# When the triangles of the delta rule are prepared: grams one group sooner, from key copies of their own, and inversion steps spread over three chunks

## The chip, the cores and the metric

The kernel runs on one core of one Trainium2 chip. The metric is the device time of one execution in microseconds (us); the table below gives the median of three runs. A core has five engines that work beside each other and wait for each other by semaphores: TensorE (PE in the profile; PEld its weight loads), VectorE (DVE), ScalarE (ACT), GpSimd (POOL) and SyncE (SP), which here only issues DMAs. Each engine takes its own instructions in order.

## The reference

Four batches of eight heads and 768 tokens (head size 48) go through the delta rule, token by token:

```python
k_n = k / (np.linalg.norm(k, axis=-1, keepdims=True) + 1e-06)
for t in range(S):
    kt, vt, bt = (k_n[:, :, t], v[:, :, t], beta[:, :, t, None])
    y[:, :, t] = np.einsum('bhd,bhde->bhe', q[:, :, t], state)
    v_old = np.einsum('bhde,bhd->bhe', state, kt)
    state = state + bt[:, :, :, None] * np.einsum('bhd,bhe->bhde', kt, vt - v_old)
```

Its result, 3072 tokens of 384 features, goes through two feed-forward layers with 2048 hidden units each: `h = x @ w_in`, a function of h (first a clipped square that becomes linear above 1, then the square of `max(h, 0)`), and `g @ w_out`. All is float32.

## The kernel before, in words

**Chunks.** The 768 tokens are cut into 24 chunks of 32 tokens; a chunk holds all batches and heads. With K the keys of a chunk, Q its queries and S the state, a chunk needs `W`, the inverse of a unit lower triangle made of `K K'`, scaled. Then U = W (diag(n) V − K S), Y = Q S + strictlower(Q K') U, and S grows by K' U. On TensorE these are six *steps*, each a burst of small matmuls: ks (K S), tr (times W), yy (Q S, line 406), sps (K' U into the state), yy again (times U, line 440) and xt (the transpose of Y for the next layer).

**Grams and triangles.** What a chunk needs before its state is known is made ahead. `gram` (line 260) computes K K' and Q K' on TensorE, and VectorE masks them into the tile `gp` (line 284). Four chunks form a *group* (0 to 5). When a group has its four grams, `tri` (line 317) inverts its 128 triangles at once, one on each partition: VectorE transposes `gp` into `gm` (line 325), a few small instructions make norms and factors, two larger ones (lines 350 and 354, each in halves on VectorE and GpSimd) prepare `gm` and `tx`, then 30 *steps* follow, each a product (`t`, line 370) and a sum (`tx`, line 376). For groups 1 to 5 all 60 are on GpSimd. A closing transpose on VectorE (line 380) puts the result into `gp`, from which tr reads it.

**The layers.** The first layer takes the chunks in nine *blocks* of 2 or 3 chunks (256 or 384 columns), the second in eight blocks of 3. A block has 16 *hidden units* of 128, each with nine matmuls `h` and nine matmuls `acc` two units later. Between the two, ScalarE and VectorE make of h the function's value and split it in a high and a low part. For each unit that is `r` (line 516), `g` (line 518) and `gl` (line 527) on VectorE, with ScalarE's `gh` (line 526) between the last two. Beside that VectorE, ScalarE and GpSimd convert weights that come as float64 bits: those of the first layer in block 0, those of the second in the later blocks (lines 158 to 164).

**What sets the order.** Each block has 32 *slots*, two for a hidden unit. The steps of a later block's chunks are spread evenly over the slots of the block before (`put_a`), and after certain steps of chunk c come grams of chunks some way ahead, read from the same key tiles (`kqt`, a ring of 6) that the chunk's own steps read later. When a group's last gram is in slot a, its triangle begins in slot a + 1; its steps are recorded in the 6 slots (`PACE`) from a + 6, and the closing transpose in the slot where the group's first chunk starts. All this is inside `manual_schedule(engines=ENGINES)` with TensorE alone in `ENGINES`: TensorE's instructions stay in the order in which they are recorded, those of the other engines are put in order by a scheduler of the language, when the kernel is built.

**Loads.** All DMAs are issued by SP, in order: keys and queries (`kqt`, two DMAs a chunk), keys and values (`kv`, ring of 3), weights (`raw`), the converted second weights out to memory (`w2f`) and, in the last block, back in (`w2r`, in the same ring as `kqt`). A chunk's values are multiplied by norms on GpSimd (`value`, line 249).

Of the kernel before, what the change touches and what calls it, by code (L numbers as in the profile page):

```python
# [8 lines left out]
F32 = mybir.dt.float32  # L9
# [9 lines left out]
# Chunks of the blocks in which the first layer takes them  # L19
SIZES = [2, 2, 3, 3, 3, 3, 3, 2, 3]  # L20
# and of the groups whose triangles are inverted together
GROUPS = [4] * 6
# [3 lines left out]
def kernel(  # L26
# [9 lines left out]
    """The delta rule in chunks of T tokens, with keys as they come (K, not normalised):  # L36
    with n = |k| + 1e-6 and g = beta / n**2,
        W = inverse(1 + diag(g) strictlower(K K')) diag(g),  U = W (diag(n) V - K S),
        Y = Q S + strictlower(Q K') U,                       S <- S + K' U.
    Its result goes through the two feed-forward layers, whose float32 products are sums of  # L40
    products of exact parts: x = hi + lo, 12 bits each (float32r).

    kq:   [chunk, (batch % 2, feature), (batch // 2, head, key tokens | query tokens)]
    kv:   [chunk, (batch, token), (key | value, head, feature)]
    beta: [(batch, chunk of the group, head), group, token]
    w1, w2: [128 hidden, in | out, partition, column], the bits of float64
    out:  [chunk, (batch, token), feature]
    """
# [12 lines left out]
    GC = T // H               # chunks of a full group  # L61
    NM = NCH // NC            # blocks of the second layer
    N = NC * P
    LAG = 2
    LENT = 28                 # weights whose bits may lie in the last weights' place
    RG = 3
    RAW = 3
    WT, WL = 3, 4
    GB = 2
    MANY = 4                  # first hidden units that may use the chunks' banks  # L70
    HEAD = 8                  # slots of the first block without steps of the second's chunks
# [17 lines left out]
    def weight(i, f):  # L89
        """(hi, lo) of hidden units f's weights: in (i = 0), out (1)."""  # L90
        if (i, f) not in pairs:
            t = wp.tile([P, 2, DM], F32R, tag=f"w{i}{f}", name=f"w{i}{f}")
            pairs[i, f] = t[:, 0], t[:, 1]
        return pairs[i, f]
# [3 lines left out]
    # Until the first layer begins, its banks serve the chunks too.  # L98
# [18 lines left out]
    def load_kq(c, tag="kqt", bufs=6):  # L117
        if c >= NCH:
            return
        t = kqt[c] = ring.tile([P, B2, H, 2 * T], F32, tag=tag, bufs=bufs, name="kqt")  # L120
        for o in range(2):
            nc.sync.dma_start(
                t[64 * o:64 * o + D].rearrange("p b h x -> p (b h x)"), kq[c, D * o:D * (o + 1)]
            )

# [6 lines left out]
    # A weight comes as the bits of a float64: words (low, high).  The high word, read as a  # L132
    # float32 and scaled by 2**-112, has its exponent rebiased; shifted left by 3 it is the
    # weight's leading 21 bits as a float32.  The low word adds the last 3 bits, rounded to
    # nearest, but never up into the leading ones.
    raws = {}

    # The last weights' place takes some of the first ones' bits.
# [8 lines left out]
    # The second layer's weights become float32.  # L147
# [22 lines left out]
    # The first layer's become their two parts, x = hi + lo.  # L170
# [14 lines left out]
    def weight_items(w):  # L185
        # A hidden unit's second weights are needed LAG units after its first.
        keys = [(w, f, i) for f in range(NF) for i in range(2)]
        if w == 0:
            keys.sort(key=lambda k: (k[1] + LAG * k[2], -k[2]))

        def item(x):
            _, f, i = keys[x]
            box = {}
            if w == 0:
                r = part_stages(keys[x], box)
            else:
                r = convert_stages(keys[x], box)
                r.append(lambda: nc.sync.dma_start(w2f[f, :, i], box["t"]))
            s1 = r[1]
            r[1] = lambda: (s1(), ahead(x + 1))  # L200
            return r

        # Loads run ahead of the conversions by the buffers there are.
        todo = list(enumerate(keys))

        def ahead(x):
            end = x + RAW
            if w == 0 and end < LENT:
                end = min(end + 2, LENT)
            while todo and todo[0][0] < end:  # L210
                load_w(*todo.pop(0))

        return lambda: ahead(0), [item(x) for x in range(len(keys))]
# [3 lines left out]
    def fetch_w2(f):  # L217
        w2r[f] = ring.tile([P, 2, DM], F32, tag="kqt", bufs=6, name="w2r")
        nc.sync.dma_start(w2r[f], w2f[f])
# [14 lines left out]
    def norm_stages(ss, sm):  # L234
        """n = sqrt(ss) + 1e-6, the root after one Newton step."""
        return [
            lambda: nc.scalar.activation(sm[0], ss, AF.Sqrt, scale=0.25, bias=tiny),
            lambda: nc.vector.reciprocal(sm[2], sm[0]),
            lambda: nc.vector.scalar_tensor_tensor(
                sm[1], ss, 0.25, sm[2], ALU.mult, ALU.mult),  # L240
            lambda: nc.vector.scalar_tensor_tensor(
                sm[0], sm[0], 1e-6, sm[1], ALU.add, ALU.add),
            lambda: nc.vector.reciprocal(sm[2], sm[0]),
        ]

    def value(c):
        """V becomes diag(n) V."""
        g, j = group_of[c]
        nc.gpsimd.tensor_mul(  # L249
            kvt[c][:, 1], kvt[c][:, 1],  # L250
            nt[g][:, j * H:(j + 1) * H].rearrange("p (h o) -> p h o", o=1)
            .to_broadcast([P, H, D]),
        )
# [6 lines left out]
    def gram(c, lo=0, hi=2, late=0):  # L260
        """K K' (x = 0) and Q K' (x = 1), x from lo to hi; what is returned is left to do
        (if late > 1, to what left its bank)."""
# [5 lines left out]
        g = att([P, H, hi - lo, T], "g")  # L268

        def one_(b, h, p, pd):  # L270
            x = kqt[c][pd, b // 2, h]
            nc.tensor.matmul(  # L272
                g[p, h].rearrange("p x i -> p (x i)"), x[:, 0:T], x[:, lo * T:hi * T],
                start=h == 0, stop=True, skip_group_check=True,
            )

        per_bh(one_)

# [16 lines left out]
    # The keys of the first chunks with the keys and queries of those after them, up to the  # L295
    # last of the first block: these do without a state.
# [13 lines left out]
    # The upper triangle of a chunk's K K', one (batch, chunk, head) a partition; its diagonal  # L310
    # is |k|**2.  x[c, i] becomes W[i, c], each of `parts` (engine, rows) by itself.
# [77 lines left out]
    us = {}  # L389

    def chunk_steps(c):
# [4 lines left out]
        def of_state(o, x):  # L396
            """K S (x = 0) or Q S; at first, S is the sum of K' U so far."""
# [32 lines left out]
        def qs():  # L430
            o = t["o"] = att([P, H, D], "yy")
            of_state(o, 1)
            if c >= HEADS:
                kqt.pop(c)
                load_kq(c + 6)
# [24 lines left out]
        def done():  # L460
            """Of ku and xt, the second makes room."""
            t["n"] = t.get("n", 0) + 1
            if t["n"] == 2:
                del kvt[c]
                load_kv(c + 3)
# [20 lines left out]
    def prods(pairs, swap=False):  # L486
        """Sums of hi hi + lo hi + hi lo, the right's lo last."""
# [11 lines left out]
    def hidden(layer, n, f):  # L499
# [12 lines left out]
        if layer == 0:  # L512
            # g = (min(relu(h + 1), 2) / 2)**2 + relu(h - 1)
# [69 lines left out]
    def flow(items, lag=1):  # L583
        """The stages of items, each item `lag` steps behind the one before it."""
# [20 lines left out]
    PACE = 6  # L605
# [9 lines left out]
    with tc.manual_schedule():  # L615
# [4 lines left out]
        load_kq(4)  # L620
        load_kq(5)
# [27 lines left out]
        for c in range(HEADS):  # L649
            load_kq(c + 6)  # L650
# [9 lines left out]
    with tc.manual_schedule(engines=ENGINES):  # L660
# [28 lines left out]
        def later(*fs):  # L689
            """These, queued behind what the hidden units need by then."""  # L690
# [9 lines left out]
        # The chunks' steps, spread evenly over the slots of the block before theirs; with them  # L700
        # the products of the chunk whose keys take the place of this one's.
        at, ready, due = {}, {}, [GFIRST[2]]
        for n in range(1, NB):
            todo = []
            for c in range(FIRST[n], FIRST[n] + SIZES[n]):
                left = {0: 1, 1: 1, 2: 0, 3: 2}[c % GC]
                for i, s_ in enumerate(chunk_steps(c)):
                    todo.append(((at, c) if i == 0 else None, s_))
                    x = due[0]
                    if i + left > 5 and x < NCH:  # L710
                        left -= 1
                        due[0] += 1
                        todo.append(((ready, x), lambda x=x: gram(x)))
            for i, (mark, s_) in enumerate(todo):
# [8 lines left out]
        def tri_put(g, a, z):  # L723
# [4 lines left out]
            a += 4  # L728
            for i, s_ in enumerate(steps):
                put(0, a + i * min(z - a, PACE) // len(steps), s_)  # L730
# [103 lines left out]
```

## Time and profile before

| | |
|---|---|
| median of 3 runs | 1115.31 us |
| lowest, highest | 1114.62, 1117.25 us |
| span of the profiled execution | 1115.4 us |
| TensorE, VectorE, ScalarE, GpSimd busy | 999.2, 649.7, 506.3, 315.9 us |
| moved by DMA | 73.00 MB |

The profile is of one execution; its span runs from its first to its last instruction, and the page gives no other time for it. The time is that of the chain that ended last, so a busy share alone says little: what is read first is which engine the others wait for in a stage, and what ended those waits. Block 0 of the first layer runs from about 78 to 165 us, blocks 1 to 8 up to about 705 us, the second layer from there to the end.

### The profile page before, as it was taken

Reading aid. Unit: us, or ns where it says so; the run is one execution under the profiler, and the core shown is the slowest. Engines: PE = TensorE matmul, PEld = TensorE weight load, DVE = VectorE, ACT = ScalarE, POOL = GpSimd, SP = SyncE. Lnnn points to the kernel's source line nnn. Section 1 sums busy time; section 2 is a strip of 40 time slices with the busy share of each in tenths; the row PEclk is TensorE's granted clock in tenths of the full one; section 3 lists DMA queues with packets and bytes.
Section 4 is the critical chain, followed back from the end, with each engine's and each line's share of the span. In section 5 each row is a group of like instructions: output and inputs, shape, how many; then the busy total and the mean of one; then the engine's idle time right before and its main releaser. Section 6 shows DMA issues by size and latency. Waiting matters only on the chain.

```text
span 1115.4 us, 32967 instructions
## 1 busy us (share of the span) xinstructions
PE 999.2 (90%) x14312; PEld 955.1 (86%) x14312; DVE 649.7 (58%) x1235; ACT 506.3 (45%) x1068; POOL 315.9 (28%) x462
## 2 busy tenths in 40 slices
PE   4344879979997999699979999899999999999998
PEld 3334879968986999699879999899999999999998
DVE  4999887765684485466654467754344343434333
ACT  1045646635553555365455666433333333333332
POOL 3477760580184029204800021311101010101000
PEclk9966889998998999899989999999999999999999
DMA  8145325133141151141211122201010010000000
GB/s 231 38 143 164 88 87 177 57 100 101 31 151 58 35 165 57 35 152 38 67 36 44 39 87 86 86 1 43 1 43 28 16 43 1 22 1 22 1 22 22
DMA packets 33489, 73.00 MB, mean 65 GB/s; under 512 B 3904, under 2 KB 17728, under 8 KB 33344
## 3 DMA queue, kind: packets, MB, share of 16 engines
q1 hardware_dynamic: 33344, 70.89, 20.9%
q8 instruction: 112, 1.84, 0.7%
q14 instruction: 33, 0.27, 0.1%
HBM read 55.15 MB, written 15.73 MB: 64 GB/s over the span
## 4 chain that ended last, share of the span: by engine, by line
PE 67%; DVE 14%; POOL 11%; issue 5%; ACT 3%; DMA 1%; SPq 0%; DVEq 0%; ACTq 0%; POOLq 0%
PE h L489 30%; PE acc L489 30%; POOL tx L376 5%; POOL t L370 5%; DVE wl L161 2%; DVE wl L158 2%; DVE g L518 2%; DVE wl L164 1%; PE tr L420 1%; PE g L272 1%; DVE tx L376 1%; PE yy L440 1%; DVE t L370 1%; PE yy L406 1%; PE ks L406 1%
## 5 line engine op out<-in xcount | busy, mean ns | idle before, releaser
L489 PE MATMUL h<-xh,w 128*128 128x384 f32 (+1 forms) x1632 | 326.2, 337 | 25.6 <-ACT g L515 25.1
L489 PEld LDWEIGHTS h<-xh,w 128*128 128x128 f32 x1632 | 277.4, 194 | 31.9 <-ACT g L515 25.1
L527 DVE TENSOR_TENSOR gl<-g,gh 128x384 fp32r<-128x384 f32 (+1 forms) x272 | 169.3, 622 | 122.2 <-ACT gh L526 117.0
L526 ACT CAST gh<-g 128x384 fp32r<-128x384 f32 (+1 forms) x272 | 134.5, 494 | 210.7 <-DVE g L518 109.8
L489 PE MATMUL h<-xl,w 128*128 128x384 f32 (+1 forms) x816 | 181.9, 332 | 2.1 <-DVE xl L477 2.1
L489 PE MATMUL acc<-gh,w 128*128 128x384 f32 (+1 forms) x864 | 171.8, 336 | 8.2 <-ACT gh L526 5.6
L521 DVE TENSOR_TENSOR g<-r 128x384 f32<-128x384 f32 x128 | 71.3, 557 | 156.8 <-ACT r L520 156.8
L489 PE MATMUL acc<-w,gh 128*128 128x384 f32 x768 | 155.5, 337 | 1.6 <-DVE e L534 1.6
L489 PEld LDWEIGHTS acc<-gh,w 128*128 128x128 f32 x864 | 140.8, 196 | 13.5 <-ACT gh L526 5.7
L520 ACT ACTIVATE r<-h,zero 128x384 f32<-128x384 f32 x128 | 74.5, 582 | 165.4 <-PE h L489 165.4
L489 PEld LDWEIGHTS h<-xl,w 128*128 128x128 f32 x816 | 143.7, 193 | 2.4 <-DVE xl L477 2.4
L489 PEld LDWEIGHTS acc<-w,gh 128*128 128x128 f32 x768 | 136.3, 188 | 1.9 <-ACT gh L526 1.9
L514 ACT ACTIVATE r<-h,one 128x384 f32<-128x384 f32 (+1 forms) x144 | 78.4, 544 | 84.1 <-PE h L489 82.1
L518 DVE TENSOR_TENSOR g<-g,r 128x384 f32<-128x384 f32 (+1 forms) x144 | 90.3, 627 | 38.3 <-ACT r L517 37.0
L516 DVE TENSOR_SCALAR r<-r 128x384 f32<-128x384 f32 (+1 forms) x144 | 60.5, 420 | 78.4 <-ACT r L514 78.0
L370 POOL TENSOR_TENSOR t<-tx,gm 128x30 f32<-128x30 f32 (+16 forms) x171 | 96.5, 564 | 15.3 <-DVE tx L354 3.5
L376 POOL TENSOR_TENSOR tx<-tx,t 128x30 f32<-128x30 f32 (+16 forms) x171 | 96.7, 565 | 11.9
L489 PE MATMUL acc<-gl,w 128*128 128x384 f32 (+1 forms) x432 | 92.5, 323 | 4.1 <-DVE gl L527 4.1
L249 POOL TENSOR_TENSOR kv<-kv,nt 128x384 f32<-128x384 f32 x24 | 21.5, 901 | 259.9 <-DMA kv<-in_kv_dram 84.6
L517 ACT ACTIVATE r<-r 128x384 f32<-128x384 f32 (+1 forms) x144 | 70.6, 490 | 48.7 <-DVE r L516 47.8
L576 POOL CAST xh<-x2r 128x1152 fp32r<-128x1152 f32 x8 | 9.5, 1187 | 293.1 <-PE h L489 293.1
L489 PE MATMUL acc<-w,gl 128*128 128x384 f32 x384 | 88.0, 337 | 0.0
(85 smaller groups left out, 1032.0 us busy)
## 6 DMA issues: line engine op xcount, KB each, us to landing
raw<-in_w_dram SPq DMA_DIRECT2D x64, 384.0 KB, 3.3
kqt<-in_kq_dram SPq DMA_DIRECT2D x48, 192.0 KB, 4.2
kv<-in_kv_dram SPq DMA_DIRECT2D x24, 384.0 KB, 3.1
w2f<-wl SPq DMA_DIRECT2D x32, 192.0 KB, 2.6
w2r<-w2f SPq DMA_DIRECT2D x16, 384.0 KB, 3.0
x2r<-x SPq DMA_DIRECT2D x8, 576.0 KB, 4.3
out_dram<-e SPq DMA_DIRECT2D x24, 192.0 KB, 1.9
x<-e SPq DMA_DIRECT2D x18, 192.0 KB, 3.6
```

Of the source, the lines that this page charges most:

```text
L158: nc.vector.tensor_scalar(bits, raw[:, :, 0].bitcast(U32), 2.0 ** -29, 7.0, ALU.mult, ALU.min)
L370: eng.tensor_mul(t, x[:, lo:hi, j:j + 1].to_broadcast([P, hi - lo, w]), gm[:, j:j + 1, j + 1:T].to_broadcast([P, hi - lo, w]),)
L376: ins = eng.tensor_add(x[:, lo:hi, j + 1:T], x[:, lo:hi, j + 1:T], t)
L489: nc.tensor.matmul(o, *((r, l) if swap else (l, r)), **flags)
L514: marks[0] = nc.scalar.activation(r, h, AF.Relu, bias=one)
L516: marks[1] = nc.vector.tensor_scalar(r, r, 2.0, 0.5, ALU.min, ALU.mult)
L517: nc.scalar.activation(r, r, AF.Square)
L518: nc.vector.tensor_add(g, g, r)
L520: marks[0] = nc.scalar.activation(r, h, AF.Relu, bias=zero)
L521: marks[1] = nc.vector.tensor_mul(g, r, r)
L526: nc.scalar.copy(ghi, g)
L527: nc.vector.tensor_sub(glo, g, ghi.bitcast(F32))
```

## The change

Grams of later groups no longer read the key tiles of the chunks' own steps. They have a ring of two copies, `kqg`, loaded for them alone; as soon as a gram has read its copy, the copy for the gram two later is asked for. The ring `kqt` shrinks from 6 to 4 tiles, which also holds for `w2r`. The four grams of group g + 1 are recorded after the second to the fifth step of the first chunk of group g; so group 2's are in block 1 (at chunk 4), where two of them were in block 0 before. The triangle's steps are recorded over the slots from its preparation to four slots ahead of the group's first chunk.

```diff
+    KQ, KG = 4, 2
...
-    def load_kq(c, tag="kqt", bufs=6):
-        if c >= NCH:
-            return
-        t = kqt[c] = ring.tile([P, B2, H, 2 * T], F32, tag=tag, bufs=bufs, name="kqt")
+    def load_kq(c):
+        if c < NCH:
+            kqt[c] = fetch_kq(c, "kqt", KQ)
+    kqg = {}
+    def load_kg(c):
+        if c < NCH and c not in kqg:
+            kqg[c] = fetch_kq(c, "kqg", KG)
+    def fetch_kq(c, tag, bufs):
+        t = ring.tile([P, B2, H, 2 * T], F32, tag=tag, bufs=bufs, name="kqt")
...
-        w2r[f] = ring.tile([P, 2, DM], F32, tag="kqt", bufs=6, name="w2r")
+        w2r[f] = ring.tile([P, 2, DM], F32, tag="kqt", bufs=KQ, name="w2r")
...
+        src = kqt[c] if c < KQ else kqg[c]
         def one_(b, h, p, pd):
-            x = kqt[c][pd, b // 2, h]
+            x = src[pd, b // 2, h]
...
         per_bh(one_)
+        if c >= KQ:
+            kqg.pop(c)
+            load_kg(c + KG)
...
                 kqt.pop(c)
-                load_kq(c + 6)
+                load_kq(c + KQ)
...
-        load_kq(4)
-        load_kq(5)
+        for c in range(KG):
+            load_kg(KQ + c)
...
         for c in range(HEADS):
-            load_kq(c + 6)
+            load_kq(c + KQ)
...
-        at, ready, due = {}, {}, [GFIRST[2]]
+        at, ready = {}, {}
         for n in range(1, NB):
             todo = []
             for c in range(FIRST[n], FIRST[n] + SIZES[n]):
-                left = {0: 1, 1: 1, 2: 0, 3: 2}[c % GC]
+                g, j = group_of[c]
+                due = []
+                if j == 0 and 1 <= g < NG - 1:
+                    due = list(range(GFIRST[g + 1], GFIRST[g + 1] + GROUPS[g + 1]))
                 for i, s_ in enumerate(chunk_steps(c)):
                     todo.append(((at, c) if i == 0 else None, s_))
-                    x = due[0]
-                    if i + left > 5 and x < NCH:
-                        left -= 1
-                        due[0] += 1
+                    if i and due:
+                        x = due.pop(0)
                         todo.append(((ready, x), lambda x=x: gram(x)))
...
-            a += 4
+            a += 3
             for i, s_ in enumerate(steps):
-                put(0, a + i * min(z - a, PACE) // len(steps), s_)
+                put(0, a + i * (z - 4 - a) // len(steps), s_)
             put(0, z, end)
```

Comments are taken out as well, and lines move by up to 17 numbers: the steps' lines 370 and 376 are 385 and 391 in the changed kernel, the transposes' 325 and 380 are 340 and 395.

Three places in the order of the instructions show what is moved. The first is TensorE around the first gram of group 2. Before, it stands in block 0 (`w_` names the weights of a unit, 256 columns wide; `xt` is the transposed result of chunk 2):

```order
L489 MATMUL h<-xh,w_2026 128x256 x6
L489 MATMUL h<-xl,w_2026 128x256 x3
L272 MATMUL g<-kqt 32x64 x32
L489 MATMUL acc_1421<-gh,w_1960 128x256 x2
...
L489 MATMUL h<-xh,w_2112 128x256 x6
L489 MATMUL h<-xl,w_2112 128x256 x3
L474 MATMUL xt<-ident,kv 128x128 x3
```

In the changed program it stands in block 1, behind the second step (tr) of chunk 4, and the next gram follows the third (yy):

```order
L435 MATMUL tr<-kv,gp 32x48 x32
L504 MATMUL h<-xh,w_988 128x256 x6
L504 MATMUL h<-xl,w_988 128x256 x3
L284 MATMUL g<-kqt 32x64 x32
...
L504 MATMUL h<-xh,w_1078 128x256 x6
L504 MATMUL h<-xl,w_1078 128x256 x3
L421 MATMUL yy<-st,kqt 32x48 x32
...
L284 MATMUL g<-kqt 32x64 x32
```

So two grams have left block 0, and the four of a group stand between the steps of one chunk.

The second is GpSimd in the middle of group 2's steps (`t` and `tx` are the product and the sum of a step, `kv<-kv,nt` a value product). Before:

```order
L370 TENSOR_TENSOR t<-tx,gm 128x220
L376 TENSOR_TENSOR tx<-tx,t 128x11x20
L370 TENSOR_TENSOR t<-tx,gm 128x228
L376 TENSOR_TENSOR tx<-tx,t 128x12x19
L249 TENSOR_TENSOR kv<-kv,nt 128x384
L370 TENSOR_TENSOR t<-tx,gm 128x234
```

The same steps in the changed program:

```order
L385 TENSOR_TENSOR t<-tx,gm 128x220
L391 TENSOR_TENSOR tx<-tx,t 128x11x20
L260 TENSOR_TENSOR kv<-kv,nt 128x384
L385 TENSOR_TENSOR t<-tx,gm 128x228
L391 TENSOR_TENSOR tx<-tx,t 128x12x19
L385 TENSOR_TENSOR t<-tx,gm 128x234
```

The value product stands one step earlier; a second one, for the next chunk, stands 11 steps behind it, where before there was none. Apart from value products nothing stands between the steps of this group in either program.

The third is VectorE around the closing transpose of group 4 (`r`, `g`, `gl` are a unit's three rows; `wl` weight conversion, `st` the state). Before:

```order
L456 COPY st<-sps_77 128x384
L527 TENSOR_TENSOR gl<-g,gh 128x384
L516 TENSOR_SCALAR r<-r 128x384
L518 TENSOR_TENSOR g<-g,r 128x384
L380 STREAM_TRANSPOSE gp<-tx 128x32x32
L527 TENSOR_TENSOR gl<-g,gh 128x384
L284 TENSOR_TENSOR gp<-g,mask 128x8x2x32
```

In the changed program:

```order
L531 TENSOR_SCALAR r<-r 128x384
L169 TENSOR_SCALAR wl<-raw 128x384
L172 SCALAR_TENSOR_TENSOR wl<-wt,wl 128x384
L471 COPY st<-sps_77 128x384
L533 TENSOR_TENSOR g<-g,r 128x384
L175 SCALAR_TENSOR_TENSOR wl<-wt,wl 128x384
L395 STREAM_TRANSPOSE gp<-tx 128x32x32
L542 TENSOR_TENSOR gl<-g,gh 128x384
```

In both the transpose stands inside a unit, between its g and its gl; the gram's mask that followed has moved elsewhere.

## Rows read from the trace of the kernel before

**Rows 1.** The page: TensorE's and the others' busy time (share of the span), instructions.

```profile
PE 999.2 (90%) x14312; PEld 955.1 (86%) x14312; DVE 649.7 (58%) x1235; ACT 506.3 (45%) x1068; POOL 315.9 (28%) x462
```

**Rows 2.** Windows, two stages: busy us of each engine, granted clock, DMA share, GB/s.

```profile
78.00:165.00 87.00, 61.39 (x1236) 56.69 (x1236) 78.54 (x122) 47.33 (x117) 65.27 (x80) 0.77 0.40 120
222.00:300.00 78.00, 69.04 (x1372) 62.96 (x1371) 45.94 (x80) 37.27 (x77) 25.13 (x41) 0.93 0.28 83
```

**Rows 3.** Waits of VectorE: us in total, times, longest us.

```profile
DVE gp L380 <- POOL tx L376: 34.8, 5, 11.7
```

**Rows 4.** Timeline of VectorE, groups 2 to 5: start, us, instruction, [idle before <-releaser].

```profile
208.12 0.68 DVE L354 TENSOR_TENSOR tx<-gm,st 128x512 f32<-128x512 f32 x1
...
248.37 2.04 DVE L380 STREAM_TRANSPOSE gp<-tx 128x1024 f32<-128x1024 f32 x1 [7.84 <-POOL tx L376]
...
305.38 1.11 DVE L354 TENSOR_TENSOR tx<-gm,st 128x512 f32<-128x512 f32 x1
...
347.66 2.02 DVE L380 STREAM_TRANSPOSE gp<-tx 128x1024 f32<-128x1024 f32 x1 [8.99 <-POOL tx L376]
...
412.99 1.10 DVE L354 TENSOR_TENSOR tx<-gm,st 128x512 f32<-128x512 f32 x1
...
454.20 2.06 DVE L380 STREAM_TRANSPOSE gp<-tx 128x1024 f32<-128x1024 f32 x1 [11.65 <-POOL tx L376]
...
517.24 1.11 DVE L354 TENSOR_TENSOR tx<-gm,st 128x512 f32<-128x512 f32 x1
...
558.33 2.06 DVE L380 STREAM_TRANSPOSE gp<-tx 128x1024 f32<-128x1024 f32 x1 [5.83 <-POOL tx L376]
```

**Rows 5.** Timeline of ScalarE behind group 2's transpose.

```profile
250.86 0.51 ACT L526 CAST gh<-g 128x384 fp32r<-128x384 f32 x1 [9.41 <-DVE g L518]
```

**Rows 6.** Timeline of TensorE behind the four transposes.

```profile
251.91 2.29 PE L489 MATMUL h<-xh,w 128*128 128x384 f32 x6 [7.96 <-ACT g L515]
...
350.81 1.93 PE L272 MATMUL g<-kqt 48*32 48x64 f32 x64 [7.08 <-DVE gp L284]
...
457.33 1.93 PE L272 MATMUL g<-kqt 48*32 48x64 f32 x64 [9.37 <-DVE gp L284]
...
563.36 2.29 PE L489 MATMUL h<-xh,w 128*128 128x384 f32 x6 [5.95 <-ACT g L515]
```

**Rows 7.** The chain that ended last, four stretches: start, us, what.

```profile
154.37 1.54 PE g L272 x64
...
160.61 1.03 PE g L272 x64
...
200.16 1.06 PE h L489 x9
201.22 0.81 PE ks L406 x64
...
214.76 0.33 PE xt L474 x3
...
251.91 3.25 PE h L489 x9
255.16 2.85 PE acc L489 x9
...
716.88 1.58 PE acc L489 x9
718.46 1.56 PE h L489 x9
```

**Rows 8.** Timeline of GpSimd: the value product between group 2's steps.

```profile
223.25 0.83 POOL L249 TENSOR_TENSOR kv<-kv,nt 128x384 f32<-128x384 f32 x1
```

**Rows 9.** Windows of GpSimd's steps on tx, groups 1 and 2: stretch, us, busy.

```profile
68.60:161.00 92.40, 38.78 (x60) 0.73 0.42 127
208.80:248.40 39.60, 34.17 (x60) 0.99 0.31 90
```

**Rows 10.** DMA issues: count, KB each, median us from issue to landing.

```profile
kqt<-in_kq_dram SPq DMA_DIRECT2D x48, 192.0 KB, 4.2
```

More of the change, by code (lines that the diff above doesn't have):

```diff
@@ L124, in load_kq @@
             )
+        return t
     def load_kv(c):
@@ L603 @@
     w1f.reverse()
-    PACE = 6
     SPREAD = 3
@@ L705 @@
             for c in range(FIRST[n], FIRST[n] + SIZES[n]):
-                left = {0: 1, 1: 1, 2: 0, 3: 2}[c % GC]
+                g, j = group_of[c]
+                due = []
+                if j == 0 and 1 <= g < NG - 1:
+                    due = list(range(GFIRST[g + 1], GFIRST[g + 1] + GROUPS[g + 1]))
                 for i, s_ in enumerate(chunk_steps(c)):
                     todo.append(((at, c) if i == 0 else None, s_))
-                    x = due[0]
-                    if i + left > 5 and x < NCH:
-                        left -= 1
-                        due[0] += 1
+                    if i and due:
+                        x = due.pop(0)
                         todo.append(((ready, x), lambda x=x: gram(x)))
+                assert not due
             for i, (mark, s_) in enumerate(todo):
```

## The prediction

> **What bounds the kernel now.** I read the page first: TensorE is busy for 999.2 of 1115.4 us [rows 1], so a change can gain only where TensorE waits or runs at its lower clock. The table by stage comes next. While the first layer takes block 0 (78 to 165 us), VectorE is busy for 78.5 of 87 us and TensorE for 61.4, at a mean granted clock of 0.77: there VectorE's weight conversions bound. In a later stage such as 222 to 300 us TensorE is busy for 69.0 of 78 us [rows 2]; what is missing there is one wait, and three more stages up to 612 us have one each.
>
> The list of waits names their source: VectorE stood in front of the closing transpose of a triangle (gp, L380) for 34.8 us in 5 waits, each time until GpSimd's last step (tx, L376) [rows 3]. The timeline gives four of them, for groups 2 to 5: 7.84, 8.99, 11.65 and 5.83 us [rows 4], 34.3 in all; the fifth, of group 1, is the rest, 0.5 us. VectorE takes its instructions in order, so everything behind the transpose stands too. ScalarE's next cast (gh) came 9.41 us late, for the g that VectorE makes after the transpose [rows 5], and TensorE stood for 7.96, 7.08, 9.37 and 5.95 us [rows 6], 30.4 us together. TensorE never waited for the inverted triangle of these groups itself; it waited because VectorE did.
>
> So a TensorE stall is VectorE's wait, plus the transpose itself (2.04 us), less the work that TensorE had in hand. That slack is 1.9, 3.9, 4.3 and 1.9 us in the four groups. After such a stall the granted clock is at its 1.2 GHz level for a while: the first unit behind group 2's takes 3.25 + 2.85 us for its two products, where a quiet one takes 1.56 + 1.58 [rows 7], so each stall costs about 3.0 us more.
>
> **The change, step by step.** *Where the closing transpose now stands.* The new code records GpSimd's 30 steps over three chunks instead of six slots, and the transpose at the end. But only TensorE's order is as recorded; the other engines' order is made by the scheduler. The changed program shows what it did. Group 3's last step is recorded in slot 108, that is in unit 54, yet VectorE's closing transpose of that group stands among its rows of unit 50. On GpSimd the steps still follow each other with nothing but value products and weight parts between them. So the steps were pulled together again, and the transpose was pulled forward behind them.
>
> What decides is therefore the work that lies between the start of the steps (VectorE's last preparation, tx, L354 before and L369 after) and the transpose in VectorE's order. Its rows r, one a hidden unit, count 8, 7, 7 and 8 before for groups 2 to 5, and 9, 7, 8 and 8 after. TensorE's work up to the last product that these rows need: a group of nine 384-column matmuls is 1.57 us, one of 256 columns 1.06, a chunk step (ks, tr, yy, sps) 0.81, a gram 1.03, a transpose of a chunk's result (xt) 0.33 [rows 7].
> - Group 2 before: 9 groups of 256, 7 of 384, 9 steps, 2 transposes, 1 gram: 9.5 + 11.0 + 7.3 + 0.7 + 1.0 = 29.5. After: 16, 2, 11, 2, 0: 17.0 + 3.1 + 8.9 + 0.7 = 29.7. So +0.2.
> - Group 3: 14 of 384, 8 steps, 1 transpose in both: 28.8, so 0.
> - Group 4 before: 14, 9, 1: 22.0 + 7.3 + 0.3 = 29.6. After: 16, 8, 1: 25.1 + 6.5 + 0.3 = 31.9. So +2.3.
> - Group 5: 16, 7, 1 before, 15, 9, 1 after: 31.1 and 31.2, so +0.1.
>
> VectorE in fact took 32.4, 33.3, 29.6 and 35.3 us from tx to its arrival at the transpose, and GpSimd was done 40.2, 42.3, 41.2 and 41.1 us after tx [rows 4]. I add the differences to the arrivals. In group 2 GpSimd has two value products between its steps where it had one, 0.83 us each [rows 8]; I take that in full. The waits become 40.2 + 0.8 − 32.6 = 8.4, then 42.3 − 33.3 = 9.0, 41.2 − 31.9 = 9.3 and 41.1 − 35.4 = 5.7: 32.4 us for 34.3. With the same slack TensorE gains **1.9 us**.
>
> *GpSimd's step time.* The 60 instructions of a group take 34.2 us in group 2, and took 38.8 for group 1, which ran beside a VectorE that was nearly full [rows 2, 9]. Group 4 will have 68 VectorE rows beside its steps for 42 before, the others fewer than before. Bounds: 0 to +4.6 us for that group; I take 0, since groups 2 to 5, between which VectorE's load differs, do not differ like that. The Trainium skill (SBUF — State Buffer, Who interferes with whom) says that a VectorE instruction with two inputs in SBUF and a GpSimd instruction that reads there shut each other out. The direction of [rows 9] agrees; by that rule the term for group 4 would be nearer its upper bound than 0.
>
> *Two grams leave block 0.* Chunks 8 and 9 had theirs at 154.37 and 160.61 us, when TensorE already worked without a gap: 1.54 + 1.03 us [rows 7]. They go into block 1, which TensorE bounds: 2 × 1.03. Net **−0.5 us**. If the waits beside them in block 0 swallow the gain it is +2.1; this end goes into the range.
>
> *More key copies.* 20 more chunk loads of keys pass SP's queue, each in two DMAs with a landing about 4.2 us after issue [rows 10]. A copy is asked for when the gram two before has been read, and a gram of the second pair stands about 2.5 to 3 units behind that (8 us and more), so I cost it at 0, hidden by those units. At the program's start grams 6 and 7 now wait for copies after grams 4 and 5; the inversion of group 0 covers that. If a copy lands late, TensorE stands at the gram. The weights and value loads queued behind it on SP come later too, and VectorE's conversions wait for weights. Bounds 0 to 8 us (four groups, two grams each, about a microsecond each).
>
> *The ring of keys of 4 instead of 6* feeds chunks that follow at over 20 us each, and in the last block weights that are fetched several units ahead: 0.
>
> Sum, against the profiled execution's span of 1115.4 us: 1115.4 − 1.9 − 0.5 = **1113.0**. The median of the runs is 1115.31, so nothing visible lies around the span. What a measurement here can tell from no change is 0.2%, 2.2 us, so the forecast lies right at that edge.
>
> **The rivals.** *The wait shrinks by more.* If GpSimd's chain is to be counted from the first transpose of a triangle (gm) and not from tx, TensorE's work up to the closing transpose grows from 34.7, 34.4, 35.2 and 36.7 us to 36.3, 34.7, 37.8 and 38.7, worked out in the same way: 6.5 us less waiting, and the shortest stall may end before the clock falls, 3.0 more. With 0.5 for the grams and 0.8 back for the value product: 1106. For it: these are the changed program's own positions. Against: part of that growth is ahead of tx, where the steps have not begun, so it is no head start.
>
> *It does what it says.* All four stalls and their clock go: 30.4 + 4 × 3.0 + 0.5 = 42.9, so 1072.5. For it: the steps are recorded 30 slots wide, ending four slots ahead of the chunk. Against: the changed order, above, undoes that. Whatever GpSimd does, VectorE reaches the transpose after some 33 us and GpSimd needs 40.
>
> *The slack goes: slower.* Place: VectorE's queue right behind the closing transpose. In groups 2 and 5 it now stands between a unit's r and g, in group 2 also ahead of the block's accumulators, which the next block needs. Before, in group 5, it stood behind a whole unit. Price: the slack of all four is 1.9 + 3.9 + 4.3 + 1.9 = 12.0 us, so at most 1125. It decides from 4.6 us of lost slack on (the 2.4 of the sum and the 2.2). Against: in group 4 the same row, gl, stands behind the transpose as before.
>
> **How the numbers follow.** The forecast case, the stalls staying nearly as they are, gets 0.48, with its own range 1109 to 1117; more shrinking 0.22, the lost slack 0.24, the full effect 0.06. About half of the forecast case is faster by over 0.2%, most of the rest within. So faster 0.24 + 0.22 + 0.06 = 0.52, said 0.50; within 0.2% 0.25; slower 0.25. The range is 1104 to 1121: down to the second case with some margin, up to two thirds of the lost slack; the full effect and the last third are left out.
>
> **What would show it.** Right, if VectorE's four waits for tx are still there, near 8.4, 9.0, 9.3 and 5.7 us, with TensorE standing 6 to 9 us behind each and the clock falling after it; and if TensorE's waits for key copies after 50 us are under 2 us in all. Wrong, if a closing transpose does not wait (the steps were spread after all), if a TensorE stall exceeds VectorE's wait plus 2 us (the slack was lost), or if a new wait at a gram for keys appears.

## The result, and the profile after

The changed kernel takes 1121.83 us (median of 4 runs, 1120.64 to 1122.84), the kernel before took 1115.81 us on the same chip: a ratio of 1.0053, with a 95% interval of 1.0038 to 1.0067. It is 6.0 us slower. The forecast was 1113.0 us, in a range of 1104 to 1121: wrong in direction, and 0.8 us above the range.

The profiled execution of the changed kernel is its fastest run: a span of 1118.9 us in 1120.64 us. The spans of the four runs reach from 1118.9 to 1121.1 us, so its trace shows 3.5 us of the 6 against the span before. The rest lies in which executions were profiled: each of these four times is 1.7 to 1.8 us above its span, so the span of 1115.4 us of the kernel before can only be that of its slowest run, 1117.25 us. The page's line that answers to [rows 1]:

```profile
PE 1003.3 (90%) x14312; PEld 954.2 (85%) x14312; DVE 644.5 (58%) x1235; ACT 506.7 (45%) x1068; POOL 316.6 (28%) x462
```

TensorE is busy 4.1 us longer with the same instructions; the page does not show where. VectorE's waits for GpSimd's last step, as in [rows 3]:

```profile
DVE gp L395 <- POOL tx L391: 35.3, 5, 9.6
```

Almost the same sum, 35.3 for 34.8 us, in as many waits; the single ones have moved. VectorE's timeline, the five transposes and the last preparation of groups 2 to 5 ([rows 4] has groups 2 to 5 of before):

```profile
160.77 2.06 DVE L395 STREAM_TRANSPOSE gp<-tx 128x1024 f32<-128x1024 f32 x1 [5.20 <-POOL tx L391]
...
198.56 0.68 DVE L369 TENSOR_TENSOR tx<-gm,st 128x512 f32<-128x512 f32 x1
...
239.09 1.99 DVE L395 STREAM_TRANSPOSE gp<-tx 128x1024 f32<-128x1024 f32 x1 [8.28 <-POOL tx L391]
...
288.92 1.10 DVE L369 TENSOR_TENSOR tx<-gm,st 128x512 f32<-128x512 f32 x1
...
329.76 2.03 DVE L395 STREAM_TRANSPOSE gp<-tx 128x1024 f32<-128x1024 f32 x1 [6.40 <-POOL tx L391]
...
391.32 0.68 DVE L369 TENSOR_TENSOR tx<-gm,st 128x512 f32<-128x512 f32 x1
...
434.06 2.02 DVE L395 STREAM_TRANSPOSE gp<-tx 128x1024 f32<-128x1024 f32 x1 [5.80 <-POOL tx L391]
...
501.59 0.68 DVE L369 TENSOR_TENSOR tx<-gm,st 128x512 f32<-128x512 f32 x1
...
541.89 2.01 DVE L395 STREAM_TRANSPOSE gp<-tx 128x1024 f32<-128x1024 f32 x1 [9.61 <-POOL tx L391]
```

The first row is new. Before, group 1's wait was 0.5 us:

```profile
160.95 2.22 DVE L380 STREAM_TRANSPOSE gp<-tx 128x1024 f32<-128x1024 f32 x1 [0.49 <-POOL tx L376]
```

There VectorE reached the transpose at 160.47 us, and GpSimd was done at 160.92. Now GpSimd is done at the same time, 160.74 us, and VectorE is there at 155.57. TensorE's stalls behind the five, of which [rows 6] has the last four of before:

```profile
163.51 1.01 PE L504 MATMUL h<-xl,w 128*128 128x256 f32 x3 [6.56 <-DVE xl L492]
...
242.33 2.29 PE L504 MATMUL acc<-gh,w 128*128 128x384 f32 x6 [10.21 <-DVE e L549]
...
334.70 2.29 PE L504 MATMUL h<-xh,w 128*128 128x384 f32 x6 [6.59 <-ACT g L530]
...
436.54 1.20 PE L504 MATMUL acc<-gl,w 128*128 128x384 f32 x3 [4.21 <-DVE gl L542]
...
544.37 1.33 PE L504 MATMUL h<-xl,w 128*128 128x384 f32 x3 [10.11 <-DVE xl L492]
```

Groups 2 to 5 cost 31.1 us of stalls, where it was 30.4; group 1 adds 6.56. The windows around the new stall (busy us of PE, PEld, DVE, ACT, POOL, then the granted clock), first of the kernel before, then of the changed one:

```profile
160.00:167.00 7.00, 6.74 (x225) 6.11 (x223) 5.63 (x11) 3.45 (x9) 1.59 (x4) 1.00 0.14 52
```

```profile
157.00:160.00 3.00, 0.00 (x0) 0.00 (x0) 0.00 (x0) 0.00 (x0) 2.45 (x8) 1.00 0.10 41
160.00:167.00 7.00, 3.49 (x72) 3.15 (x73) 4.72 (x8) 2.40 (x6) 1.37 (x4) 0.52 0.00 1
```

From 157 to 160 us only GpSimd works, and what follows runs at the 1.2 GHz level (0.52). The start of a hidden unit (ScalarE's first row of it) shows where the time is lost. Each entry is the start in one profiled execution less that in the kernel before, so it is good to about 2 us. Unit 12 is in block 0, unit 16 opens block 1, and the runs in the lower lines are those of the next section:

```
unit        12     16     20     40     64     80    104    end
after     -6.5   -0.4   +4.3   +4.9   +5.2   -0.9   +3.5   +3.5
b_g1      -5.0   +0.9   +5.7   +7.0   +6.9   +6.9   +6.9   +6.9
a_end1b   -5.8   -6.8   +2.7   +4.1   +4.6   -1.4   +3.4   +3.3
a_end1    -5.3   -6.4   -1.8   +0.1   +0.7   -5.1   -0.2   -0.3
a_g0      -0.5   -0.7   -0.3   +2.0   +2.7   -3.3   +1.6   +1.9
b_copies   0.0    0.0    0.0   -1.6   -0.8   -0.3   -0.2   -0.3
```

Block 0 runs 6.5 us ahead by unit 12, has lost that by unit 16, and is 4.3 us behind at unit 20. From there to the end the kernel loses nothing more (-0.8): group 4 gains 6, group 5 gives 4 back.

### The profile page after: what moved, and what is told of

Read it like the earlier page. It is cut to its first block, busy times and chain, and to the rows that moved or that the text cites. A ratio compares the mean times of both kernels' runs of the same rounds, so it can differ in the third digit from the quotient of the medians.

```text
span 1118.9 us, 33038 instructions
## 1 busy us (share of the span) xinstructions
PE 1003.3 (90%) x14312; PEld 954.2 (85%) x14312; DVE 644.5 (58%) x1235; ACT 506.7 (45%) x1068; POOL 316.6 (28%) x462
## 4 chain that ended last, share of the span: by engine, by line
PE 62%; DVE 14%; POOL 13%; issue 5%; ACT 3%; DMA 1%; SPq 0%; DVEq 0%; POOLq 0%; ACTq 0%
PE acc L504 28%; PE h L504 28%; POOL t L385 6%; POOL tx L391 6%; DVE g L533 2%; DVE wl L169 1%; DVE wl L175 1%; DVE wl L172 1%; PE g L284 1%; DVE t L385 1%; DVE tx L391 1%; DVE gl L542 1%; PE yy L455 1%; PE tr L435 1%; PE ks L421 1%
```

## The experiments

The theory ahead of them: VectorE stands at transposes that are placed too early in its order; the new wait of group 1 eats up what block 0 gained. Rival 1: the copies, SP's queue and the smaller ring. Rival 2: the two grams' own 2.06 us in block 1. Rival 3: the spread of the steps. Each ratio is against the kernel before, run on the same chip.

**Later transposes.** `later` is the kernel's own helper: it ties an instruction behind two marks of the unit in which it is recorded, ScalarE's first row and VectorE's row r of that unit (`SL` is 32, the slots of a block). a_late uses it for groups 2 to 5, a_late1 for group 1, the two kernels named "all" for both.

```diff
a_late:
-            put(0, z, end)
+            put(0, z, *later(end))
a_late1:
-        end1()
...
+        put(0, SL - 1, *later(end1))
```

> The changed kernel with the closing transposes of groups 2 to 5 placed later in VectorE's order (behind units 36, 56, 80 and 104 counted over the blocks, instead of 30 to 33, 50, 72 and 95); group 1's stays. Theory: VectorE's four waits of 8.28, 6.40, 5.80 and 9.61 us fall below 1 us each, TensorE's stalls of 10.21, 6.59, 4.21 and 10.11 us go (31.1 us), and about 2.5 to 3 us of lower clock behind each: 1078 to 1083 us; group 1's stall of 6.6 us stays. Rival (TensorE would have waited for the inverted triangle at its step tr, or for the next late thing, anyway): tr of the group's first chunk now waits, and no more than 10 us come back, 1110 us or more.

Measured: 1085.33 us, ratio 0.9717 (0.9704 to 0.9731). The theory's direction and nearly its size, 2 us above its range. No transpose of groups 2 to 5 waits any more; the first row is group 1's, the second one of the other four:

```profile
161.51 2.06 DVE L395 STREAM_TRANSPOSE gp<-tx 128x1024 f32<-128x1024 f32 x1 [5.20 <-POOL tx L391]
...
243.75 2.23 DVE L395 STREAM_TRANSPOSE gp<-tx 128x1024 f32<-128x1024 f32 x1
```

> The changed kernel with one thing moved: the closing transpose of group 1's triangle stands one hidden unit further back in VectorE's order (behind the rows of unit 15 of block 0 instead of unit 14); every transfer, gram and GpSimd step stays. Theory (VectorE stands at a transpose that is placed too early; group 1's wait of 5.2 us is new because block 0 lost two grams and runs ahead while GpSimd is done at the same time): the wait is gone or under 1 us, TensorE's new stall of 6.56 us at 163.5 us goes, and with it most of the stretch at the lower clock behind it (160 to 167 us): 8 to 10 us less, 1112 to 1114 us, so slightly under the kernel before. Rival 1 (the copies and SP's queue cost the time) and rival 2 (it is the two grams that went from a block which VectorE bounds into one which TensorE bounds): group 1's wait only uses up time that was to spare, 1120 to 1123 us.

Measured: 1123.74 us, ratio 1.0065 (1.0051 to 1.0079): no gain. But the test failed as a test: the edit moved the transpose past a single row r, and VectorE still waited.

```profile
161.34 2.04 DVE L395 STREAM_TRANSPOSE gp<-tx 128x1024 f32<-128x1024 f32 x1 [4.70 <-POOL tx L391]
```

> The changed kernel with the transposes of all five groups later. Theory: both gains add, 31.1 + 6.6 us of stalls and some 14 us of lower clock behind five of them: 1069 to 1074 us. Rival (the two gains are the same idle time, used up by another limit): not under the kernel in which groups 2 to 5 alone are moved by more than 2 us.

Measured: 1085.07 us, 0.9717 (0.9702 to 0.9732), 11 us above what was expected and the same as a_late, since group 1's wait (4.70 us) was still there, as in a_late1.

> The kernel before with the transposes of all five groups later in VectorE's order. Theory: its four stalls of 7.96, 7.08, 9.37 and 5.95 us go, with some 11 us of lower clock: 1073 to 1077 us; and it stands within 5 us of the changed kernel with the same move, since the copies, the place of the grams and the spread of the steps do nothing by themselves. Rival 1 (copies and SP's queue cost the 6.5 us): it is 6 us or more faster than the changed kernel with the same move.

Measured: 1089.45 us, 0.9751 (0.9736 to 0.9767), 12 us above its range. With transposes out of the way the changed kernel is the faster of the two, by 4.4 us, against rival 1. Group 2 shows a reason: the kernel before begins its triangle 5 units later, and TensorE's tr then waits for the triangle itself (groups 3 and 4 have such waits too, 1.69 and 3.00 us).

```profile
252.96 1.50 PE L420 MATMUL tr<-kv,gp 32*32 32x48 f32 x64 [6.32 <-DVE kv L416]
```

**The parts one by one.** b_copies is the kernel before with copies and the smaller ring alone; a_pace undoes the spread; b_g1 is the kernel before with the grams of chunks 8 and 9 in block 1, which also moves the chunk steps that share their slots, and nothing else; a_g0 undoes that move in the changed kernel.

```diff
b_g1:
                 left = {0: 1, 1: 1, 2: 0, 3: 2}[c % GC]
+                left = {3: 0, 4: 3}.get(c, left)
a_g0:
-                    due = list(range(GFIRST[g + 1], GFIRST[g + 1] + GROUPS[g + 1]))
+                    due = list(range(GFIRST[g + 1] + 2 * (g == 1), GFIRST[g + 1] + GROUPS[g + 1]))
+                early2 = [8, 9] if c == 3 else []
...
+                    if i >= 4 and early2:
+                        x = early2.pop(0)
+                        todo.append(((ready, x), lambda x=x: gram(x)))
a_pace (and b_copies, with the order of grams of before):
-            a += 3
+            a += 4
             for i, s_ in enumerate(steps):
-                put(0, a + i * (z - 4 - a) // len(steps), s_)
+                put(0, a + i * min(z - a, 6) // len(steps), s_)
```

> The copies by themselves: the kernel before with its own places of the grams, steps and transposes, but grams that read key copies of their own (ring of 2) and a key ring of 4. Theory: TensorE waits for key copies only in the first 50 us, as it did for key tiles; 1114 to 1118 us, within 2 of the kernel before. Rival 1 (copies, SP's queue or the smaller ring cost the 6 us): 1120 us or more, with waits for copies or weights that the kernel before does not have.

Measured: 1116.52 us, ratio 1.0003 (0.9994 to 1.0011): nothing. Rival 1 is out.

> The changed kernel with the inversion steps recorded over six slots again, as before. Theory: the scheduler puts GpSimd's steps and the transposes in the same places either way: 1120 to 1124 us, as the changed kernel. Rival 3 (the spread itself costs the time): 1114 to 1118 us.

Measured: 1122.92 us, 1.0060 (1.0046 to 1.0075), as the changed kernel. Rival 3 is out.

> The kernel before with one thing changed: the grams of chunks 8 and 9 stand in block 1 instead of block 0; no copies, no spread, and the transposes of groups 2 to 5 at their old places among the units. Theory: this alone brings group 1's wait: VectorE reaches the transpose some 5 us before GpSimd is done, TensorE stands for 6 to 7 us near 163 us, the clock falls, and the two grams cost 2.06 us in block 1: 1120 to 1123 us, as the changed kernel. Rival (the loss comes from later groups): 1114.5 to 1118.5 us, the two grams at most.

Measured: 1123.88 us, 1.0066 (1.0052 to 1.0080). This one move makes the whole loss, with the same wait and the same stall, while groups 3 to 5 stay as they were (table above: +7.0 at unit 40, +6.9 at the end). VectorE, then TensorE:

```profile
162.03 2.06 DVE L380 STREAM_TRANSPOSE gp<-tx 128x1024 f32<-128x1024 f32 x1 [5.21 <-POOL tx L376]
```

```profile
164.76 1.01 PE L489 MATMUL h<-xl,w 128*128 128x256 f32 x3 [6.55 <-DVE xl L477]
```

> The changed kernel with the grams of chunks 8 and 9 back in block 0, as before; the copies, the other places and the spread stay. Theory: VectorE reaches group 1's transpose at about 160 us again and waits for under 1 us, TensorE's stall at 163 us and the lower clock behind it go, and block 1 has two grams fewer: unit 20 starts no more than 1.5 us behind the kernel before, where it was 4 to 6 behind: 1116 to 1119 us. Rival 2 (only the price of the two grams in a block which TensorE bounds counts): 2.06 us less, 1119.5 to 1120.5 us. Rival 1 (copies): no change, 1120 to 1124 us.

Measured: 1119.91 us, 1.0033 (1.0021 to 1.0045), 2 to 3 us less than the changed kernel, 1 us above the theory's range and inside that of rival 2. The trace tells the two apart. Up to unit 20 the theory came true: VectorE waits 1.67 us, TensorE stands 1.41 us in front of tr instead of 6.56, and the unit is 0.3 us ahead. Then 2.8 us are lost up to unit 28, in al_g0 2.9. Up to 202 us TensorE waits there three times, 0.40, 1.08 and 1.07 us (in al_g0 1.13, 0.46 and 1.07), where the kernel before has one wait of 0.28. At the second, ScalarE has stood 1.58 us for VectorE's row r, which comes behind the preparation of group 2's triangle:

```profile
187.98 0.95 PE L504 MATMUL h<-xh,w 128*128 128x256 f32 x6 [1.08 <-ACT g L530]
```

So preparing that triangle in the middle of block 1 costs this wait. What the other two come from was not followed.

**Group 1's wait taken apart.** a_end1 and a_end1b record group 1's transpose two slots and one slot further than a_late1.

```diff
a_end1:
+        put(0, SL + 1, *later(end1))
a_end1b:
+        put(0, SL + 0, *later(end1))
```

> The changed kernel with group 1's closing transpose two hidden units back in VectorE's order, behind the gl of unit 16 (the earlier attempt moved it past a single row r, VectorE still waited there for 4.7 us, and nothing was gained). Theory (block 0 runs ahead without its two grams, and group 1's wait with its lower clock eats that up): VectorE waits there for under 1.5 us; TensorE's stall of 6.56 us becomes 2 to 3 us in front of the tr of chunk 4, which needs the transpose and cannot come before some 163 us: 1115 to 1119 us, 3 to 6 less than the changed kernel. Rivals (copies and SP's queue; the two grams in block 1; the spread of the steps): nothing changes, 1120 to 1124 us.

Measured: 1115.69 us, 0.9997 (0.9987 to 1.0007): all of the loss is gone. It has the two grams in block 1, so their own price (rival 2) does not make the loss. But in this kernel tr of chunk 4 stands ahead of the transpose and reads the triangle before its inversion. So it shows the time without any wait for group 1's triangle, not only without VectorE's. TensorE's timeline, ks and tr, with tr 7 us earlier than in the changed kernel, then VectorE's transpose:

```profile
158.41 0.88 PE L421 MATMUL ks<-st,kqt 48*32 48x48 f32 x64
...
160.48 0.88 PE L435 MATMUL tr<-kv,gp 32*32 32x48 f32 x64
```

```profile
162.56 2.18 DVE L395 STREAM_TRANSPOSE gp<-tx 128x1024 f32<-128x1024 f32 x1 [0.88 <-POOL tx L391]
```

> The changed kernel with group 1's closing transpose behind the r of unit 16 and ahead of the kv of chunk 4's first product, so that the tr of chunk 4 reads the inverted triangle. In the earlier run a_end1 the transpose stood behind that tr, which therefore read the triangle before its inversion; that run shows what the wait costs when nothing at all takes its place. Theory: VectorE arrives at about 160.5 us and waits for about 1 us; TensorE then waits in front of tr itself, since tr needs the transpose (done at about 163): 2.5 to 3.5 us instead of the 6.56 us, with little of the lower clock behind it: 1117 to 1120 us, 2 to 5 less than the changed kernel. Rival (the gain of a_end1 was that of tr not waiting, not of VectorE's queue): 1121 to 1123 us.

Measured: 1120.18 us, 1.0033 (1.0020 to 1.0045), between theory and rival, just outside the theory's range. VectorE waits 2.62 us, and TensorE stands in front of tr, which needs the transpose and the kv behind it:

```profile
164.30 1.50 PE L435 MATMUL tr<-kv,gp 32*32 32x48 f32 x64 [4.22 <-DVE kv L431]
```

So the queue behind VectorE's wait is some 2 us of the 6; the rest is the triangle that is not there, and the kv behind it. At unit 20 the three kernels stand at +4.3 (VectorE waits early), +2.7 (tr waits) and -1.8 (tr does not wait). The intervals of the changed kernel and of a_end1b overlap, so the 2 us rest on the traces too: unit 20 stands at +4.3 to +5.8 in all eight kernels in which VectorE still waits there for 4.7 to 5.2 us, and at +2.7 and +1.3 in a_end1b and al_end1b.

**What stands behind a transpose.** a_s25 moves the transposes of groups 2 and 5 back by one unit; a_s25p does the same with the steps over six slots.

```diff
-            put(0, z, end)
+            if g in (2, 5):
+                put(0, {2: 68, 5: 192}[g], *later(end))
+            else:
+                put(0, z, end)
```

> The changed kernel with the closing transposes of groups 2 and 5 one hidden unit further back in VectorE's order: group 2's behind the copies of the block's accumulators and the gl of unit 33, group 5's behind xl, g and gl of unit 95. Theory (what stands right behind the transpose sets the slack): VectorE's waits fall from 8.3 and 9.6 us by the length of a unit, to 4 to 5.5 us each, and TensorE's stalls by more, from 10.2 and 10.1 to 2 to 4 us, since the work that it needs next is out already: 1105 to 1111 us. Rival (the stall is the wait, whatever stands behind the transpose): stalls of 6 to 7.5 us, 1112 to 1117 us.

Measured: 1110.31 us, 0.9947 (0.9934 to 0.9959). Group 5's transpose was recorded amid its own steps here and taken after 39 of 60, so its time is not that of a kernel that computes all, and only group 2's wait and stall count (5.85 and 5.40 us).

> The same move of the transposes of groups 2 and 5 as in the run before, now with the steps recorded over six slots (which by itself changed nothing), so that all 60 instructions of group 5 stand ahead of its transpose; in the run before, that transpose was taken after 39 of them, and its figures for group 5 say nothing. Theory: group 2 as there (wait 5.9, stall 5.4 us); group 5's wait falls from 9.6 to 10.3 us by a unit to 5 to 6 us, its stall from 10.1 to 10.9 to 2 to 4 us, since xl, g and gl of unit 95 are out by then: 1109 to 1113 us. Rival (the stall is the wait, whatever stands behind the transpose): group 5's stall falls by no more than the wait, to 5.5 us or more: 1112 to 1116 us.

Measured: 1115.55 us, 0.9993 (0.9985 to 1.0002), in the rival's range; a_pace, which differs in these two transposes alone, has 1.0060. The waits, then the stalls:

```profile
241.17 2.02 DVE L395 STREAM_TRANSPOSE gp<-tx 128x1024 f32<-128x1024 f32 x1 [5.83 <-POOL tx L391]
...
541.03 2.01 DVE L395 STREAM_TRANSPOSE gp<-tx 128x1024 f32<-128x1024 f32 x1 [6.40 <-POOL tx L391]
```

```profile
245.37 0.90 PE L489 MATMUL xt<-ident,kv 128*128 128x128 f32 x3 [5.41 <-ACT kv L459]
...
543.50 1.50 PE L435 MATMUL tr<-kv,gp 32*32 32x48 f32 x64 [5.90 <-DVE kv L431]
```

In group 2 the wait fell by 2.4 us and the stall by 4.8: its slack came back, though not to the 2 to 4 us of stall that was expected. In group 5 the wait fell by 3.2 and the stall by 4.2; the rival's figure (5.5 us or more) held there, since tr stood next. What stands behind counts, by 1 to 2.4 us.

**Both together.** al_end1 is a_end1 with the late transposes of a_late, al_end1b a_end1b with them, al_g0 is a_g0 with them.

> The version that the runs point to: the changed kernel with all five closing transposes behind the work that TensorE needs next (groups 2 to 5 as in the run that moved them alone, group 1's behind unit 16). Theory: the 6 us of group 1 come off the 1085.3 us of that run: 1078 to 1081 us. Rival (the two gains are one): 1084 to 1087 us.

Measured: 1076.43 us, 0.9642 (0.9629 to 0.9655); tr of chunk 4 reads the uninverted triangle here too, so this is an end that no full kernel reaches in this way.

> The same place for group 1's transpose, with those of groups 2 to 5 as in a_late. Theory: the same 2 to 5 us come off the 1085.3 us of a_late: 1080 to 1083.5 us. Rival: 1084 to 1086 us.

Measured: 1081.84 us, 0.9692 (0.9678 to 0.9705), as the theory said: with al_g0, whose interval overlaps, the fastest kernel that computes all. Its stretch of 222 to 300 us, where the changed kernel has TensorE busy for 67.30 us at 0.93:

```profile
222.00:300.00 78.00, 76.75 (x1665) 70.03 (x1664) 55.45 (x100) 42.94 (x90) 39.69 (x65) 1.00 0.36 109
```

> a_late with the grams of chunks 8 and 9 back in block 0. Theory: block 0 has no lead that is lost at group 1's transpose (wait 1.7 us in a_g0), block 1 has two grams fewer, and group 2's earlier start no longer costs what it cost in a_g0, because its transpose stands late: unit 20 is 5 to 6 us earlier than in a_late, 1079 to 1081 us, the fastest of all with a full inversion. Rival (the two grams are worth their own 2.06 us at most, the wait nothing): 1083 to 1085 us.

Measured: 1082.50 us, 0.9698 (0.9685 to 0.9711), 1.5 us above the theory and just under the rival's range, with the three waits told of at a_g0.

## Why the prediction was wrong

**The step that failed: "Two grams leave block 0", net -0.5 us, with +2.1 as the other end.** b_g1 does this alone and costs 7.3 us. Three things were left out. (1) Moving two grams also moves the steps of chunks 2 and 3, which share the slots with them: ks of chunk 3 goes from unit 9 to unit 10 and xt from 14 to 15. Block 0 ran 6.5 us ahead by unit 12. That lead is not the grams': before, unit 12 starts at 151.19 us, ahead of both (154.37 and 160.61 us, [rows 7]). So it comes with the moved steps; no run moves the grams without them, and how they bring it was not followed.

```profile
151.19 0.48 ACT L514 ACTIVATE r<-h,one 128x256 f32<-128x256 f32 x1
```

(2) Little of that lead can be used. GpSimd's steps of group 1 end at 160.7 us as before, since they do not depend on TensorE, and tr of chunk 4 needs that triangle. In a_end1b, where GpSimd is done at 161.8, tr starts at 164.30 us, 2.0 us sooner than before; with GpSimd done at 160.7 and nothing but the transpose (2.06 us) in between it would be 162.8, an estimate, or 3.5 us sooner. (3) VectorE, which arrived 0.5 us ahead of GpSimd, now arrives 5.2 us ahead, and everything behind its transpose stands; the first work after that runs at the lower clock. So tr starts 1.4 us later than before. The first row is of the kernel before, the second of the changed one:

```profile
166.29 0.88 PE L420 MATMUL tr<-kv,gp 32*32 32x48 f32 x64 [0.27 <-DVE kv L416]
```

```profile
167.66 0.88 PE L435 MATMUL tr<-kv,gp 32*32 32x48 f32 x64
```

After that come the two grams' 2.06 us; the other 1.6 us up to unit 28 (5.0 us behind) are not accounted for. I carried group 1's wait over as "0.5 us, the rest", and worked out new waits for groups 2 to 5 alone. The rows for it were there: [rows 9] ends group 1's steps at 161 us, and an earlier VectorE could only wait longer.

**Where the closing transpose stands: right.** The steps were not spread (a_pace), the four waits are there, and each is ended by GpSimd. Forecast 8.4, 9.0, 9.3, 5.7; measured 8.28, 6.40, 5.80, 9.61: 30.1 us for 32.4. Group 2 is right; groups 3 to 5 are off by -2.6, -3.5 and +3.9, so that the sum comes this close is luck. VectorE took 32.3, 34.4, 36.9 and 30.7 us from tx to the transpose, where the added-up rows said 32.6, 33.3, 31.9 and 35.4: a count of TensorE's work says little of single arrivals.

**"With the same slack" failed too.** Slack (wait plus transpose less stall) is 0.1, 1.8, 3.6 and 1.5 us, where 1.9, 3.9, 4.3 and 1.9 were carried over. These 5.0 us are the mechanism of the third rival, and past its 4.6 us, most of it in groups 2 and 3. It ate the 4.2 us by which the four waits shrank, so that the stalls of these groups rose by 0.8 us instead of falling by 1.9. It did not make the kernel slower by itself: from unit 20 to the end the changed kernel gains 0.8 us in spite of it.

**GpSimd's step time.** Bounds 0 to 4.6 us for group 4, taken as 0. The windows on the steps, groups 1, 2 and 4 (stretch, us, busy), which answer to [rows 9]; the last row is group 4 of the kernel before:

```profile
68.30:160.75 92.45, 37.92 (x60) 0.78 0.40 127
199.30:239.07 39.77, 33.60 (x60) 0.95 0.29 81
...
392.00:434.03 42.03, 36.32 (x60) 1.00 0.44 138
```

```profile
413.70:454.20 40.50, 34.70 (x60) 0.98 0.22 67
```

Group 4 takes 1.6 us more than before, and GpSimd was done 42.7 us after tx, where 41.2 was carried over: the term is 1.5 us. The direction fits the Trainium skill (SBUF — State Buffer, Who interferes with whom), which was cited for it. The size does not: 1.5 us is nearer to 0 than to the upper bound of 4.6.

**Key copies and the ring of 4: right at 0.** b_copies shows it, and the waits for key copies, 8.1 us in 7 where there were 6.3 in 5, all lie in the first 36 us:

```profile
PE g L284 <- DMA kqt<-in_kq_dram: 8.1, 7, 3.8
```

**"It does what it says"** needed the transposes late, not the steps spread: a_late took 36.5 us off the changed kernel, and is 31.2 us under the kernel before, where that rival had priced 42.9. Its clock term was too large: the four stalls are 31.1 us, and tr has two new ones of 2.5 us together, so 7.9 us are left for the clock, an estimate of 2.0 us a stall and not 3.0.

**The base of the sum.** The forecast took the median as lying at the span. The time of a run is 1.7 us above its span, and the trace before is of the slowest of three runs; the two nearly cancel, so this moved nothing.

## What to carry to other kernels

Where work is taken out of a stage, work out every wait in it anew, the near-zero ones first: a wait of 0.5 us says that two engines arrive together, and the one that gets faster then waits by all that it gained. Look for the value that the next stage needs first and for the engine that makes it; its end bounds what the stage can gain. In an engine that takes its work in order, the place of a waiting instruction matters more than the start of what it waits for: here the late place was worth 36 us in the changed kernel, and the two grams moved from block 0 to block 1, with the steps around them, cost 7.

## What was not expected of the hardware

A stall of 4.2 us was enough for the clock to fall. The windows, first of the changed kernel behind its 6.56 us, then of a_end1b behind its 4.22 us:

```profile
160.20:167.00 6.80, 3.49 (x72) 3.15 (x73) 4.72 (x8) 2.40 (x6) 1.25 (x3) 0.50 0.00 1
```

```profile
163.30:170.10 6.80, 5.80 (x138) 5.29 (x139) 3.15 (x9) 2.13 (x5) 0.00 (x0) 0.51 0.01 2
```

Both are at the 1.2 GHz level. The changed kernel still stands until 163.51 us in its stretch, so 3.49 us of work fall into it; a_end1b works from 164.30 us on, and 5.80 us do. So the shorter stall gave back less than its difference: the fall came later and met more work. Where TensorE has no stall in front of the triangle (a_end1) the granted clock is 1.00 from 160 to 175 us.

The same program's spans differed by up to 2.2 us (1118.9 to 1121.1), so a difference of a few us between two traces has to be placed by unit before it is explained; the repeated runs, not the one trace, gave its size.
